# Four small tiles move ahead of the operands, a query tile gets its own place, and the first part's order gets 110 corrections

## The chip, the cores and the metric

The kernel runs on one core of a Trainium2 chip. Its time is the device time of one execution in microseconds (us), and a comparison is between medians of several executions. TensorE multiplies matrices, VectorE (DVE) and ScalarE (ACT) work on elements, GpSimd (POOL) only makes constants here, and SyncE (SP) issues every transfer between HBM and SBUF, in the order of its instruction list. An engine runs its own list in order too, and waits on semaphores for the others.

## The reference

Attention with pooled keys and values, and then a softplus feed-forward net, all in float32:

```python
k_p = k.reshape(B, H, Sp, 8, D).mean(axis=3)      # q, k, v: 8 x 8 x 576 x 64; Sp = 72
v_p = v.reshape(B, H, Sp, 8, D).mean(axis=3)
scores = 1/sqrt(D) * matmul(q, k_p.transpose(0, 1, 3, 2))
attn = exp(scores - max(scores)); attn = attn / (sum(attn) + 1e-9)
x = matmul(attn, v_p).transpose(0, 2, 1, 3).reshape(4608, 512)
h = x @ w_in                                      # 512 x 2048
g = maximum(h, 0) + log1p(exp(-abs(h)))
out = g @ w_out                                   # 2048 x 512
```

The inputs q, k, v and w_in are scaled by 8.

## The kernel before, in words

The 4608 tokens are taken in 18 chunks of 256, each of two tiles of 128 (class `Tile`). A batch has 576 tokens, so a chunk can lie in two batches. A float32 operand of the large products is split into a high part (type float32r) and a low part, and a product is three matmuls: high by high, low by high, high by low. The feed-forward net has two products for each chunk. In the first ("h" in the rows, line 494, `ffn1_products`) a 128 x 128 block of w_in is loaded as weights and x streams through, 256 columns; a pair u of two blocks of 128 hidden units takes 24 such matmuls. In the second product g is loaded and w_out streams: 512 columns in the early chunks ("acc", lines 516 and 576), and from chunk NF = 4 on ("m", line 684, `pair2_fast`) seven products of 256 columns for each pair u, with sums of quarters of g ("so") and combinations of quarters of w_out ("t"), 21 matmuls a pair.

The program has two parts, each ordered by the planner `Order`. A step is an `op`: an engine, an estimated cost, a function that emits instructions, the steps it comes after, and the `Slot`s (buffers, PSUM banks) that it needs. `run` gives each step a rank, its cost and the longest way to the end of what follows it. Then it picks step by step: of those that can start within 0.4 us of the earliest on the engine that would finish first, the one with the largest rank plus `first`. `first` is a bonus given by hand. The planner's times decide only the order; on the chip the engines wait for what they need.

The first part (`batch`, `weights`, `attend`, `feed`, `keys_values`, `combinations`) does chunks 0 to 2 and the attention of chunk 3, and meanwhile converts the 16 weight sets of w_in and w_out. `weights(f)` loads a set by SP (lines 757 and 760), and VectorE takes out its parts in six steps (`bits`, `clamp`, `shift`, `sign`, `lowest`, `rest`, lines 791 to 822) with one copy by ScalarE (`high`, line 818). `batch(b)` loads and pools keys and values for batches 0 and 1: keys in two halves (line 867, summed by TensorE on line 921), what is left over of both (lines 855 and 880), the transposes of the keys (line 219). `attend(c)` loads q of a chunk by tiles (line 308), transposes it (line 337), makes scores (line 357), their least value mn (line 364), exponentials with their sums sm (line 382), the normalized probabilities pm and pe (`norm`, lines 392 to 406), their transposes (lines 420 and 432), and x from the values (lines 461 to 478). `feed(c)` makes the two products of a chunk.

The second part does the steady chunks: in each pair u the first products of one pair, the second products of the pair before, and between them the attention of the next chunk. Weights of w_in are loaded again there from a copy in HBM (`load_wi`), and the combinations t by `load_t` through `load_sums`.

Buffers in SBUF have tags, and all tiles with one tag share its place. Places of a pool follow one another in the order in which the tags are first used, each rounded up to 32 bytes in a partition. The pools come in the order const, wpool (weights), one (nearly all else), two. In the pool `two` there are the tags mn and sm, with two places of 32 bytes each. Modulo 256, all weights begin at byte 192, and x, g, gh, gl and so at byte 0; between them lies the tile pe, whose 832 bytes are an odd multiple of 64.

Chunk 0's q lies in a tile that chunks 1 and 2 use after it; the load for chunk c comes after the transposes of the same tile of chunk c - 1 (`q_free[c - 1, t]`). There are four places "ld" of 4096 bytes (L, X4, X5, X6) for loads of keys, values and late weights.

Of the kernel before, what the change touches and what calls it, by code (L numbers as in the profile page):

```python
# [103 lines left out]
def pooled_attention_softplus_ffn(  # L104
# [19 lines left out]
    T = 2  # L124
# [14 lines left out]
    one = ctx.enter_context(tc.tile_pool(name="one", bufs=1))  # L139
    two = ctx.enter_context(tc.tile_pool(name="two", bufs=2))  # L140
    psum = ctx.enter_context(tc.tile_pool(name="psum", bufs=1, space=PSUM))
    dram = ctx.enter_context(tc.tile_pool(name="dram", bufs=1, space=bass.MemoryType.DRAM))
    BANKS = [f"b{i}" for i in range(8)]
    acc_banks, h_banks, at_banks, m_banks = [], [], [], []

    def spin(tags, shape, dtype, name):

        tags.append(tags.pop(0))
        return one.tile(shape, dtype, tag=tags[-1], name=name)

# [90 lines left out]
    def kv(b):  # L241

        engine = nc.vector
        kp, vp, st_ = [], [], {}

        def k_load(i, s):
            st = st_["k", i] = staging([SP, 2, POOL, D], "kst", s)
            nc.sync.dma_start(
                out=st, in_=k[b, 2 * i:2 * i + 2].rearrange("h (j s) d -> j h s d", s=POOL))

        def k_pool(i):
            if i == 0:
                kp.append(one.tile([SP, H, D], F32, tag="kp", name="kp"))
            tree(st_.pop(("k", i)), kp[0][:, 2 * i:2 * i + 2], engine)

        def v_load(i, s):
            st = st_["v", i] = staging([P, 2, POOL, D], "vst", s)
            for j in range(2):
                src = v[b, 4 * i + 2 * j:4 * i + 2 * j + 2].rearrange("e (y s) d -> y e s d", s=POOL)
                nc.sync.dma_start(out=st[j * KM:(j + 1) * KM], in_=src[0:KM])  # L260

        def v_pool(i):
            if i == 0:
# [25 lines left out]

# [39 lines left out]
    class Tile:  # L329
# [11 lines left out]

        def qT_out(self, ps):
            self.q = spin(Q, [P, HP, P], F32, "qT")
            nc.scalar.copy(out=self.q, in_=ps.rearrange("p (m i) -> p m i", m=HP))
# [14 lines left out]

        def least(self, j, ps):  # L360
# [15 lines left out]

        def exp_sum(self, j, ps):
# [7 lines left out]

        def sum(self):
            self.sm = two.tile([P, H], F32, tag="sm", name="sm")
            nc.vector.tensor_reduce(out=self.sm, in_=e_[self.c][:, self.t], axis=AX.X, op=ALU.add)
# [129 lines left out]

    def copy_out(c, t, tag=None):
        o = one.tile([P, DM], F32, tag=tag, name="o") if tag else spin(O, [P, DM], F32, "o")  # L520
        if t % 2 == 0:
# [185 lines left out]
    def load_wi(c, u):  # L707

        for k in range(2):
# [5 lines left out]

    kinds = {"bank": BANKS, "ld": LD, "ct": ["T0"], "kv": "a", "wg": "ab", "o": "ab", "qT": "ab", "mn": "ab",
             "sm": "ab", "E0": "a", "E1": "a", "pm": "a", "pe": "a", "kp": "a", "vp": "a", "lt_": "a",
             "pT": "a", "g": ["G0", "G1"], "gh": "ab", "gl": "ab", "h": "ab", **{x: "a" for x in late[:NS]}}
# [23 lines left out]
    def weights(f):  # L742
# [5 lines left out]
        def load(i):  # L748
            def fn():
# [8 lines left out]
                else:  # L758
                    for r in range(2):
# [22 lines left out]
        def bits(k):  # L782
# [5 lines left out]
            else:  # L788
                g = x["g", k] = spin(O, [P, 1, 4 * P], I32, "wg")
                up = x["raw", k].unsqueeze(1).rearrange("p x (n w) -> p x n w", w=2)[:, :, :, 1]  # L790
# [56 lines left out]
    def batch(b):  # L847
# [102 lines left out]
    def attend(c):  # L950
        s_lt, s_pT = Slot("lt_"), Slot("pT")
        lows, e_c = [], []
        tiles = [Tile(c, t) for t in range(T)]
        o_q, subs = [], []
        for t in range(T):
            def load(t=t):
                if 0 < c < N1:
                    qt_[c] = qt_[0]
                elif c not in qt_:
                    new_q(c)  # L960
                load_q_tile(c, t)
            o_q.append(op(SYNC, 1.4, load,
                          [] if c == 0 else [q_free[c - 1, t]] if c < N1 else
                          [q_free[c - 1, i] for i in range(T)], lag=2.4))
        norms = []
        for t, x in enumerate(tiles):
# [8 lines left out]
            o = op(ACT, act(512), lambda x=x, s=s_q: x.qT_out(s.tile), [o], [s_q, s_qT])  # L975
            ends, ss = [], [Slot("bank"), Slot("bank")]
# [3 lines left out]
            for i, s in enumerate(ss):  # L980
                d = op(DVE, 0.46, lambda x=x, i=i, s=s: x.least(i, s.tile), [p, *ends],
                       [s, s_mn])
                if c < N1:
                    def exp_sum(x=x, i=i, s=s, e=s_E[0], t=t):
# [4 lines left out]
                        x.exp_sum(i, s.tile)  # L989
                    ends.append(op(ACT, 1.2, exp_sum, [d], [s, s_mn, s_sm, *s_E], table="exp"))  # L990
# [13 lines left out]
        for x, ends, s_E, s_sm, s_pm, s_pe in norms:  # L1004
            if c == N1:
                ends = [op(DVE, 0.75, x.sum, [ex], [s_sm])]
            o = op(DVE, 1.45, x.norm, ends, [*s_E, s_sm, s_pm, s_pe])
# [21 lines left out]
    def feed(c):  # L1029
# [21 lines left out]
        if c < N1 - 1:  # L1051
            for t in range(T):
                s = Slot("o")
                h = {}

                def copy(t=t, h=h):
                    h["o"] = copy_out(c, t)
                o = op(DVE if t % 2 else ACT, 0.65, copy, [before2], [s, acc_slots[c][t]])
# [73 lines left out]
    for u in range(U1):  # L1132
        combinations(u)
    with tc.manual_schedule(engines={ACT, DVE, PE, SYNC}):
        for o in todo.run():
            o.fn()
# [6 lines left out]
    kinds = {"h": other[:2], "acc": other[2:4], "bank": other[4:], "ld": LD, "q": "a", "pT": "a", "qT": "ab", "lt_": "a",  # L1143
             "pe": "a", "mn": "ab", "sm": "ab", "E": "a", "kp": "a", "vp": "a", "S": "ab", "x": "b",
# [16 lines left out]
    def steady_attention(c):  # L1161
# [8 lines left out]
        for x in tiles:  # L1170
# [4 lines left out]
            qT_done[c].append(o)  # L1175
            o = op(ACT, act(512), lambda x=x, s=s: x.qT_out(s.tile), [o], [s, s_qT])
            last, ss = [], [Slot("bank"), Slot("bank")]
# [3 lines left out]
            for i, s in enumerate(ss):  # L1181
                last = [op(DVE, 0.46, lambda x=x, i=i, s=s: x.least(i, s.tile), [p, *last],
                           [s, s_mn])]
# [8 lines left out]
    def probabilities(c, tiles, s_E, s_lt, subs, where):  # L1192
# [4 lines left out]
        for x in tiles:  # L1197
            s_sm, s_pm, s_pe = Slot("sm"), Slot("G"), Slot("pe")
            o = op(DVE, 0.76, x.sum, [ex], [s_E, s_sm])
            o = op(DVE, 0.38, x.reciprocal, [o], [s_sm])  # L1200
# [189 lines left out]
```

## Time and profile before

| | |
|---|---|
| median of 3 runs | 917.85 us (916.7 to 921.63) |
| profiled execution | 915.2 us |
| its span, first to last instruction | 913.5 us |
| mean granted clock of TensorE | 0.994 |
| TensorE busy | 888.3 us (97%) |
| VectorE busy | 648.7 us (71%) |
| ScalarE busy | 407.3 us (45%) |
| moved by DMA | 191.12 MB, 209 GB/s |

A row of groups has line, engine, operation, out<-in, the sizes and the count, then busy us and mean ns of one, then idle time ahead of the group and what ended it. PE is TensorE's matmuls, PEld its weight loads, SPq the issuing of transfers. Because matmuls are pipelined, the mean of one is its latency; the distance between starts, or the lengths in the chain of waits, gives the rate. In that chain each row has start, length and what ran or was waited for, in order of time.

### The profile page before, as it was taken

The page shows a single profiled execution, that of the slowest core. Times are in us where ns is not written, and L with a number is a line of the kernel's source. Part 1 is how long each engine was busy: PE and PEld are TensorE (multiplying, and loading weights), DVE is VectorE, ACT ScalarE, POOL GpSimd, SP SyncE. Part 2 cuts the span into 40 slices and gives each one's busy share as a digit, 9 for nine tenths or more (in the row PEclk, how much of TensorE's full clock was granted, in tenths as well). Part 3 has the DMA queues.
Part 4 walks back from the last instruction along what each step waited for, and adds up shares of the span by engine and source line. Part 5 has one row for each costly group of instructions (what it writes and reads, how often), then busy time and mean ns, then how long its engine had stood idle before and what let it go on. Part 6 is the DMA issues. An engine that isn't in the chain of part 4 may idle for free.

```text
span 913.5 us, 20504 instructions
## 1 busy us (share of the span) xinstructions
PE 888.3 (97%) x8304; PEld 842.9 (92%) x8304; DVE 648.7 (71%) x1600; ACT 407.3 (45%) x824; POOL 2.4 (0%) x19
## 2 busy tenths in 40 slices
PE   4899999999999999999999999999999999999997
PEld 2678989888899999999999999999999999999997
DVE  4799988867877767787777755787666565747454
ACT  4765433344354544444353535453535343434332
POOL 1000000000000000000000000000000000000000
PEclk9899999999999999999999999999999999999999
DMA  8974625545789679789868866687656565746572
GB/s 234 265 255 144 211 93 187 153 158 155 261 288 270 215 208 249 222 256 238 236 208 243 245 201 198 215 252 223 222 168 222 192 208 184 230 144 233 161 238 84
DMA packets 107085, 191.12 MB, mean 209 GB/s; under 512 B 46064, under 2 KB 60400, under 8 KB 106992
## 3 DMA queue, kind: packets, MB, share of 16 engines
q1 hardware_dynamic: 106992, 189.82, 68.0%
q8 instruction: 65, 1.06, 0.5%
q14 instruction: 28, 0.23, 0.1%
HBM read 167.25 MB, written 22.54 MB: 208 GB/s over the span
## 4 chain that ended last, share of the span: by engine, by line
PE 94%; DVE 3%; DMA 1%; ACT 0%; issue 0%; SPq 0%; DVEq 0%; ACTq 0%
PE h L494 43%; PE m L684 30%; PE acc L516 7%; PE sc L357 3%; PE acc L576 3%; PE avp L461 2%; PE qTp L337 2%; PE avp L468 1%; PE ptp L420 1%; PE ltp L432 1%; DMA kvst<-in_k_dram 1%; PE kps L921 1%; DMA kvl<-in_v_dram 1%; DVE pm L397 0%; PE kvlp L880 0%
## 5 line engine op out<-in xcount | busy, mean ns | idle before, releaser
L494 PE MATMUL h<-x,w 128*128 128x256 f32 x3456 | 430.2, 279 | 0.7 <-DVE w L822 0.7
L494 PEld LDWEIGHTS h<-x,w 128*128 128x128 f32 x3456 | 414.9, 188 | 4.1 <-DVE w L822 0.9
L543 ACT ACTIVATE g<-h 128x512 f32<-128x512 f32 x120 | 71.8, 598 | 279.3 <-PE h L494 278.7
L684 PE MATMUL m<-w,so 128*128 128x256 f32 x1344 | 172.6, 278 | 0.0
L684 PEld LDWEIGHTS m<-w,so 128*128 128x128 f32 x1344 | 162.6, 188 | 0.0
L684 PE MATMUL m<-w,gh 128*128 128x256 f32 x672 | 131.9, 285 | 0.0
L594 DVE TENSOR_TENSOR sf<-g 128x128 f32<-128x128 f32 x112 | 32.8, 293 | 130.3 <-ACT g L543 129.4
L684 PEld LDWEIGHTS m<-w,gh 128*128 128x128 f32 x672 | 101.9, 188 | 1.9
L608 ACT CAST so<-sf 128x512 fp32r<-128x512 f32 x112 | 69.7, 622 | 55.4 <-DVE sf L597 54.9
L684 PE MATMUL m<-w,gl 128*128 128x256 f32 x336 | 93.7, 279 | 0.0
L613 DVE TENSOR_TENSOR so<-sf,so 128x512 fp32r<-128x512 f32 x112 | 77.4, 691 | 21.9 <-ACT so L608 21.7
L564 DVE TENSOR_TENSOR gl<-g,gh 128x384 fp32r<-128x384 f32 (+1 forms) x120 | 67.3, 561 | 0.6 <-ACT gh L557 0.5
L684 PEld LDWEIGHTS m<-w,gl 128*128 128x128 f32 x336 | 63.1, 188 | 0.0
L516 PE MATMUL acc<-w,g 128*128 128x512 f32 x192 | 60.8, 397 | 0.5 <-ACT g L499 0.5
L557 ACT ACTIVATE gh<-h 128x384 fp32r<-128x384 f32 (+1 forms) x120 | 59.2, 493 | 0.0
L499 ACT ACTIVATE g<-h 128x256 fp32r<-128x256 f32 x96 | 31.7, 382 | 59.0 <-PE h L494 52.8
L705 DVE TENSOR_TENSOR o<-o,m 128x256 f32<-128x256 f32 x98 | 39.7, 418 | 3.4 <-ACT o L697 0.6
L516 PEld LDWEIGHTS acc<-w,g 128*128 128x128 f32 x192 | 33.9, 187 | 6.9 <-ACT g L499 0.7
L364 DVE TENSOR_REDUCE mn<-sc 128x4 f32<-128x288 f32 x72 | 31.2, 452 | 10.6 <-PE sc L357 10.4
L516 PE MATMUL acc<-w,gl 128*128 128x512 f32 x96 | 38.0, 396 | 0.0
L597 DVE TENSOR_TENSOR sf<-g,sf 128x128 f32<-128x128 f32 x112 | 32.7, 292 | 3.9
L406 DVE TENSOR_TENSOR pe<-E,sm 128x96 f32<-128x96 f32 x72 | 15.2, 253 | 25.8 <-PE ltp L432 25.8
(165 smaller groups left out, 930.3 us busy)
## 6 DMA issues: line engine op xcount, KB each, us to landing
w<-wi SPq DMA_DIRECT2D x224, 512.0 KB
out_dram<-o SPq DMA_DIRECT2D x36, 256.0 KB
q<-in_q_dram SPq DMA_DIRECT2D x32, 256.0 KB
wst<-in_moe_w_in_dram SPq DMA_DIRECT2D x32, 256.0 KB
wst<-in_moe_w_out_dram SPq DMA_DIRECT2D x16, 512.0 KB
wi<-w SPq DMA_DIRECT2D x16, 512.0 KB
kst<-in_k_dram SPq DMA_DIRECT2D x24, 288.0 KB
vst<-in_v_dram SPq DMA_DIRECT2D x24, 256.0 KB
```

Source lines behind the costliest of these rows:

```text
L494: nc.tensor.matmul(out=ps[:, 0:CT], lhsT=row(w, kc), rhs=x[:, kc], start=first and kc == j == 0, stop=last and kc == KC - 1 and j == 2)
L499: nc.scalar.activation(out=g, in_=ps[:, 0:CT], func=AF.Softplus)
L516: nc.tensor.matmul(out=accs[c][t], lhsT=a[:, ts], rhs=w, start=f == 0 and j == 0, stop=f == FC - 1 and j == 2)
L543: nc.scalar.activation(out=g, in_=x.rearrange("p (b i) -> p b i", i=P), func=AF.Softplus)
L557: nc.scalar.activation(out=gh, in_=quarters(c, x.rearrange("p (b i) -> p b i", i=P)), func=AF.Softplus)
L564: nc.vector.tensor_tensor(out=gl, in0=quarters(c, g), in1=gh.bitcast(F32), op=ALU.subtract)
L594: tt(out=sf[:, 2], in0=g[:, 0], in1=g[:, 2], op=ALU.add)
L597: tt(out=sf[:, 3], in0=g[:, 3], in1=sf[:, 1], op=ALU.subtract)
L608: nc.scalar.copy(out=so[:, 0], in_=ss[c, u])
L613: nc.vector.tensor_tensor(out=so[:, 1], in0=sf, in1=so[:, 0].bitcast(F32), op=ALU.subtract)
L684: nc.tensor.matmul(out=ms[c][n], lhsT=x, rhs=y, start=u == 0 and j == 0 and n in (1, 6, 5, 4), stop=u == FP - 1 and j == 2 and n in (2, 7, ...
L705: nc.vector.tensor_tensor(out=o, in0=in0, in1=m[n], op=how)
```

## The change

Five things are changed.

- The pool `two` goes. mn and sm get tags mna, mnb, sma and smb in the pool `one`, 32 bytes each, chosen by the planner's slots. The rotating lists (`spin`) for qT, o and wg go too; the planner's slot names give the tags.
- The load of chunk 1's q takes an "ld" slot of its own and comes after nothing. Chunk 2 uses chunk 0's tile, after chunk 0's transposes (`q_free[0, t]`).
- Costs of SP steps for weights, keys and values are 1.5 in place of 1.75; SP begins at 0.8, and the table "exp" counts as loaded at the start.
- `HASTE` adds a number to `first` of 110 of the first part's steps, by index.
- In the second part `load_sums` loses `first=500`.

```diff
-    two = ctx.enter_context(tc.tile_pool(name="two", bufs=2))
-    def spin(tags, shape, dtype, name):
-        tags.append(tags.pop(0))
-        return one.tile(shape, dtype, tag=tags[-1], name=name)
...
-                self.mn = two.tile([P, 2, HP], F32, tag="mn", name="mn")
+                self.mn = one.tile([P, 2, HP], F32, tag="mn" + tag, name="mn")
...
-                self.sm = two.tile([P, H], F32, tag="sm", name="sm")
+                self.sm = one.tile([P, H], F32, tag="sm" + tag, name="sm")
...
+    todo.begin, todo.table = {SYNC: 0.8}, "exp"
...
-            return op(SYNC, 1.75, fn, slots=[stages[0 if early else i]], lag=2.2)
+            return op(SYNC, 1.5, fn, slots=[stages[0 if early else i]], lag=2.2)
...
-        o_k = [op(SYNC, 1.75, load(k, i), slots=[st[i]], lag=2.2) for i in range(2)]
-        o_v = [op(SYNC, 1.75, load(v, i), slots=[vt[i] or vt[0]], lag=2.2) for i in range(2)]
+        o_k = [op(SYNC, 1.5, load(k, i), slots=[st[i]], lag=2.2) for i in range(2)]
+        o_v = [op(SYNC, 1.5, load(v, i), slots=[vt[i] or vt[0]], lag=2.2) for i in range(2)]
...
-        o_q, subs = [], []
+        o_q, subs, s_q1 = [], [], Slot("ld")
         for t in range(T):
             def load(t=t):
-                if 0 < c < N1:
+                if c == 1 and c not in qt_:
+                    qt_[c] = one.tile([P, T, H, D], F32, tag=s_q1.name, name="q")
+                elif c == 2:
                     qt_[c] = qt_[0]
...
             o_q.append(op(SYNC, 1.4, load,
-                          [] if c == 0 else [q_free[c - 1, t]] if c < N1 else
-                          [q_free[c - 1, i] for i in range(T)], lag=2.4))
+                          [] if c < 2 else [q_free[0, t]] if c < N1 else
+                          [q_free[c - 1, i] for i in range(T)], [s_q1] if c == 1 else [], lag=2.4))
...
-                   [o_q[t], *([av[c - 1]] if c == N1 else [])], [s_q])
+                   [o_q[t], *([av[c - 1]] if c == N1 else [])], [s_q, *([s_q1] if c == 1 else [])])
...
+    HASTE = {27: -130, 29: -3, 34: -120, 36: -120, 45: 40, 46: 20, 48: -180, 55: -2, 56: -10,
+             57: -450, 58: 20, 62: -10, 64: 200, 72: -4, 73: -10, 77: -50, 82: -20, 93: 80, 94:
...
+             575: -140, 583: 30, 610: -20, 620: 4, 635: -80, 638: -310, 641: 40}
+    for i, x in HASTE.items():
+        todo.ops[i].first += x
...
-               lag=2.4, first=500))
+               lag=2.4))
```

More of the change, by code (lines that the diff above doesn't have):

```diff
@@ L251, in k_pool @@
         def k_pool(i):
-            if i == 0:
+            if not kp:
                 kp.append(one.tile([SP, H, D], F32, tag="kp", name="kp"))
@@ L262, in v_pool @@
         def v_pool(i):
-            if i == 0:
+            if not vp:
                 vp.append(one.tile([P, HP, D], F32, tag="vp", name="vp"))
@@ L340, in qT, with qT_out @@
                     identity=ident)
-        def qT_out(self, ps):
-            self.q = spin(Q, [P, HP, P], F32, "qT")
+        def qT_out(self, ps, tag):
+            self.q = one.tile([P, HP, P], F32, tag=tag, name="qT")
             nc.scalar.copy(out=self.q, in_=ps.rearrange("p (m i) -> p m i", m=HP))
@@ L358, in scores, with least @@
                                          rhs=kT[b % 2][js, m], start=True, stop=True)
-        def least(self, j, ps):
+        def least(self, j, ps, tag):
             if j == 0:
-                self.mn = two.tile([P, 2, HP], F32, tag="mn", name="mn")
+                self.mn = one.tile([P, 2, HP], F32, tag="mn" + tag, name="mn")
             nc.vector.tensor_reduce(out=self.mn[:, j], in_=self.view(ps), axis=AX.X, op=ALU.min)
@@ L375, in less, with exp_sum @@
                     [P, 2, 2, SP]), op=ALU.subtract)
-        def exp_sum(self, j, ps):
+        def exp_sum(self, j, ps, tag):
             if j == 0:
-                self.sm = two.tile([P, H], F32, tag="sm", name="sm")
+                self.sm = one.tile([P, H], F32, tag="sm" + tag, name="sm")
             for m in range(HP):
@@ L384, in exp_sum, with sum @@
                                      accum_out=self.sm[:, h:h + 1])
-        def sum(self):
-            self.sm = two.tile([P, H], F32, tag="sm", name="sm")
+        def sum(self, tag):
+            self.sm = one.tile([P, H], F32, tag="sm" + tag, name="sm")
             nc.vector.tensor_reduce(out=self.sm, in_=e_[self.c][:, self.t], axis=AX.X, op=ALU.add)
@@ L517, in ffn2, with copy_out @@
                                  start=f == 0 and j == 0, stop=f == FC - 1 and j == 2)
-    def copy_out(c, t, tag=None):
-        o = one.tile([P, DM], F32, tag=tag, name="o") if tag else spin(O, [P, DM], F32, "o")
+    def copy_out(c, t, tag):
+        o = one.tile([P, DM], F32, tag=tag, name="o")
         if t % 2 == 0:
@@ L713, in load_wi @@
             wi[f] = w[:, 0], w[:, 1]
-    kinds = {"bank": BANKS, "ld": LD, "ct": ["T0"], "kv": "a", "wg": "ab", "o": "ab", "qT": "ab", "mn": "ab",
+    kinds = {"bank": BANKS, "ld": LD, "ct": ["T0"], "kv": "a", "wg": "ab", "o": O, "qT": Q, "mn": "ab",
              "sm": "ab", "E0": "a", "E1": "a", "pm": "a", "pe": "a", "kp": "a", "vp": "a", "lt_": "a",
@@ L788, in bits @@
             else:
-                g = x["g", k] = spin(O, [P, 1, 4 * P], I32, "wg")
+                g = x["g", k] = one.tile([P, 1, 4 * P], I32, tag=gslot[k].name, name="wg")
                 up = x["raw", k].unsqueeze(1).rearrange("p x (n w) -> p x n w", w=2)[:, :, :, 1]
@@ L972, in attend @@
             o = op(PE, 0.5, lambda x=x, s=s_q: x.qT(bank(s, "qTp")),
-                   [o_q[t], *([av[c - 1]] if c == N1 else [])], [s_q])
+                   [o_q[t], *([av[c - 1]] if c == N1 else [])], [s_q, *([s_q1] if c == 1 else [])])
             q_free[c, t] = o
-            o = op(ACT, act(512), lambda x=x, s=s_q: x.qT_out(s.tile), [o], [s_q, s_qT])
+            o = op(ACT, act(512), lambda x=x, s=s_q, n=s_qT: x.qT_out(s.tile, n.name), [o], [s_q, s_qT])
             ends, ss = [], [Slot("bank"), Slot("bank")]
@@ L980, in attend, with exp_sum @@
             for i, s in enumerate(ss):
-                d = op(DVE, 0.46, lambda x=x, i=i, s=s: x.least(i, s.tile), [p, *ends],
+                d = op(DVE, 0.46, lambda x=x, i=i, s=s, n=s_mn: x.least(i, s.tile, n.name), [p, *ends],
                        [s, s_mn])
                 if c < N1:
-                    def exp_sum(x=x, i=i, s=s, e=s_E[0], t=t):
+                    def exp_sum(x=x, i=i, s=s, e=s_E[0], t=t, n=s_sm):
                         if c == 0 and 0 not in e_:
@@ L988, in exp_sum @@
                         x.slot = e.name
-                        x.exp_sum(i, s.tile)
+                        x.exp_sum(i, s.tile, n.name)
                     ends.append(op(ACT, 1.2, exp_sum, [d], [s, s_mn, s_sm, *s_E], table="exp"))
@@ L1005, in attend @@
             if c == N1:
-                ends = [op(DVE, 0.75, x.sum, [ex], [s_sm])]
+                ends = [op(DVE, 0.75, lambda x=x, n=s_sm: x.sum(n.name), [ex], [s_sm])]
             o = op(DVE, 1.45, x.norm, ends, [*s_E, s_sm, s_pm, s_pe])
@@ L1054, in feed, with copy @@
                 h = {}
-                def copy(t=t, h=h):
-                    h["o"] = copy_out(c, t)
+                def copy(t=t, h=h, s=s):
+                    h["o"] = copy_out(c, t, s.name)
                 o = op(DVE if t % 2 else ACT, 0.65, copy, [before2], [s, acc_slots[c][t]])
@@ L1142, in pooled_attention_softplus_ffn @@
     other = [b for b in BANKS if b not in acc_banks]
-    kinds = {"h": other[:2], "acc": other[2:4], "bank": other[4:], "ld": LD, "q": "a", "pT": "a", "qT": "ab", "lt_": "a",
+    kinds = {"h": other[:2], "acc": other[2:4], "bank": other[4:], "ld": LD, "q": "a", "pT": "a", "qT": Q, "lt_": "a",
              "pe": "a", "mn": "ab", "sm": "ab", "E": "a", "kp": "a", "vp": "a", "S": "ab", "x": "b",
@@ L1175, in steady_attention @@
             qT_done[c].append(o)
-            o = op(ACT, act(512), lambda x=x, s=s: x.qT_out(s.tile), [o], [s, s_qT])
+            o = op(ACT, act(512), lambda x=x, s=s, n=s_qT: x.qT_out(s.tile, n.name),
+                   [o], [s, s_qT])
             last, ss = [], [Slot("bank"), Slot("bank")]
@@ L1181, in steady_attention @@
             for i, s in enumerate(ss):
-                last = [op(DVE, 0.46, lambda x=x, i=i, s=s: x.least(i, s.tile), [p, *last],
+                last = [op(DVE, 0.46, lambda x=x, i=i, s=s, n=s_mn: x.least(i, s.tile, n.name), [p, *last],
                            [s, s_mn])]
@@ L1198, in probabilities @@
             s_sm, s_pm, s_pe = Slot("sm"), Slot("G"), Slot("pe")
-            o = op(DVE, 0.76, x.sum, [ex], [s_E, s_sm])
+            o = op(DVE, 0.76, lambda x=x, n=s_sm: x.sum(n.name), [ex], [s_E, s_sm])
             o = op(DVE, 0.38, x.reciprocal, [o], [s_sm])
```

10 rows, old and new, of the table HASTE are left out of this document.

## The prediction

> **What bounds the kernel now.** The page of the profile comes first: the busy row of the engines and the chain that ended last, in a span of 913.5 us.
>
> ```profile
> PE 888.3 (97%) x8304; PEld 842.9 (92%) x8304; DVE 648.7 (71%) x1600; ACT 407.3 (45%) x824; POOL 2.4 (0%) x19
> ...
> PE 94%; DVE 3%; DMA 1%; ACT 0%; issue 0%; SPq 0%; DVEq 0%; ACTq 0%
> ```
>
> TensorE is the bound: 94% of the chain is its own work. Time can come only from its idle 25.2 us (913.5 - 888.3) or from the rate of its matmuls. A table of stages shows where the idle part is (columns: busy us of each engine with instruction counts, granted clock, DMA share, GB/s).
>
> ```profile
> 0.00:55.00 55.00, 37.49 (x419) 26.70 (x419) 35.22 (x75) 34.78 (x135) 2.37 (x19) 0.91 0.88 240
> 55.00:82.00 27.00, 24.87 (x239) 21.24 (x239) 25.00 (x47) 14.18 (x27) 0.00 (x0) 1.00 0.60 195
> 82.00:905.00 823.00, 822.22 (x7620) 791.50 (x7618) 584.16 (x1470) 357.39 (x661) 0.00 (x0) 1.00 0.68 209
> 905.00:913.50 8.50, 3.69 (x32) 3.49 (x30) 4.33 (x11) 0.99 (x2) 0.00 (x0) 0.96 0.16 62
> ```
>
> Idle is 17.5 us before 55 and 2.1 us from 55 to 82, then 0.8 us up to 905; the last 4.8 us are the output's tail, which the change leaves alone. So the first part's list works on at most 19.6 us, and the 823 us from 82 to 905 answer only to the matmul rate. What the first 82 us wait for, by groups (the last column is idle time before the group and its releaser):
>
> ```profile
> L921 PE MATMUL kps<-kvst,zm 128*64 128x256 f32 x20 | 7.8, 540 | 9.6 <-DVE kvst L914 6.0 <-DMA kvst<-in_k_dram 3.7
> L357 PE MATMUL sc<-kT,qT 64*64 64x72 f32 x256 | 6.7, 252 | 1.6 <-ACT kT L225 1.6
> ...
> L337 PE MATMUL qTp<-ident,q 128*128 128x128 f32 x32 | 4.8, 286 | 1.5 <-DMA q<-in_q_dram 1.5
> ...
> L432 PE MATMUL ltp<-ident,pe 128*96 128x128 f32 x16 | 3.2, 281 | 4.9 <-DVE pe L406 4.9
> ```
>
> The 6.0 is the start (first data, then VectorE's sums) and stays. The 3.7, 1.5 and 1.6 us hang on transfers and keys, the 4.9 us on VectorE. The chain over this stretch says why the 3.7 us wait ends so late:
>
> ```profile
> 12.82 0.37 SPq L308
> 13.19 0.05 issue
> 13.24 0.88 SPq L757
> 14.11 0.05 issue
> 14.16 6.41 DMA kvst<-in_k_dram
> 20.57 0.14 issue
> 20.70 3.65 PE kps L921 x8
> ```
>
> It runs through the DMA queue's load of chunk 1's q (L308) to the key load of batch 1, for which TensorE waits until 20.70.
>
> **Part 1: chunk 1's q gets a place of its own.** Before, it reuses chunk 0's tile, so its load waits for q_free[0, t], the transposes. SP issues in order:
>
> ```profile
> 6.15 1.75 SPq L760 DMA_DIRECT2D wst<-in_moe_w_in_dram  x2
> 12.07 1.11 SPq L308 DMA_DIRECT2D q<-in_q_dram  x2
> ```
>
> SP stands still from 7.90 (6.15 + 1.75) to 12.07, 4.2 us, and behind it wait the w_out half of weight set 0, both key halves of batch 1, batch 0's values and batch 1's leftovers. The transfers themselves ran dry meanwhile (last but one column):
>
> ```profile
> 8.00:10.00 2.00, 1.79 (x2) 0.32 (x2) 0.00 (x0) 0.00 (x0) 0.00 (x0) 1.00 1.26 243
> 10.00:12.00 2.00, 2.00 (x9) 1.07 (x9) 1.37 (x2) 0.58 (x1) 0.00 (x0) 1.00 0.45 142
> 12.00:14.00 2.00, 1.76 (x69) 1.52 (x72) 0.20 (x1) 1.90 (x5) 0.00 (x0) 1.00 0.35 80
> ```
>
> Against 1.26 the two middle stretches left (0.81 + 0.91) x 2 / 1.26 = 2.7 us of transfer time unused. So everything behind that load lands 2.7 to 4.2 us earlier: 2.7 if the engines are the limit, 4.2 if the queue is. The new place is one of the four "ld" slots. Three hold batch 0's key halves and leftovers, and q of chunk 1 is the fourth, so batch 1's loads now wait for the products that read batch 0's halves out of theirs; that is why I take 3.0 us, near the lower end. It counts in full as far as the path through 20.70 goes on to the first weights: VectorE too waits on this queue, 2.81 us for the w_out of set 0:
>
> ```profile
> 19.12 0.69 DVE L791 TENSOR_SCALAR wg<-wst 128x1024 int32<-128x1024 int32 x1 [2.81 <-DMA wst<-in_moe_w_out_dram]
> ...
> 20.89 0.69 DVE L397 TENSOR_TENSOR pm<-E,sm 128x512 f32<-128x512 f32 x1
> ...
> 28.18 1.23 DVE L813 SCALAR_TENSOR_TENSOR wg<-wst,wg 128x1024 int32<-128x1024 int32 x1
> ```
>
> If that cover is gone, because another transfer takes the freed time, the part is worth 0.
>
> **Part 2: corrections to the ranks (HASTE), with the load costs 1.75 to 1.5, the queue's start at 0.8 and the "exp" table taken as loaded.** No instruction is added or removed; only the order of the first part's steps changes. By index, 27, 34 and 36 are batch 1's leftover products, first key products and key transposes on TensorE (-130, -120, -120), so chunk 0's attention goes ahead of them. Now it goes behind: its first probabilities are written at 20.89 (above), and TensorE transposes them here, ten microseconds later:
>
> ```profile
> 31.04 0.60 PE L420 MATMUL ptp<-ident,pm 128*128 128x128 f32 x4
> ```
>
> Most other entries reorder VectorE's six conversion steps of a weight set against the attention and the split of g. What they can win is the idle time left once part 1 is in: 4.9 + 1.6 = 6.5 us. Not all of it: VectorE is busy 25.00 of 27 us from 55 to 82, so there only its order can change, not its amount. I take 3.0 us, somewhat under half. The bounds are 6.5 us gained, and 2.5 us lost, if two of VectorE's long steps (1.23 us each, L813 above) get in front of a normalization that TensorE waits for.
>
> **Part 3: addresses.** The two mn and two sm tiles, 32 bytes each, leave the last pool and get their place at their first use, in chunk 0's attention: ahead of lt_, pT, x, g, gh, gl and so. These move up by 4 x 32 = 128 bytes; the weights, in an earlier pool, stay. Modulo 256 the weights begin at 192 and x, g and the sums at 0, so 64 above; after, at 128, 64 below. In the first products the weights are loaded and x streams, in the second ones g or so is loaded and weights stream: the two kinds have opposite signs already. A steady chunk in the chain (start, length):
>
> ```profile
> 497.21 2.83 PE h L494 x24
> 500.04 2.39 PE m L684 x21
> 502.43 2.72 PE h L494 x24
> 505.16 2.48 PE m L684 x21
> ...
> 541.97 2.48 PE m L684 x21
> 544.45 0.59 PE h L494 x5
> ```
>
> Identical runs have two lengths: 2.83 or 2.72 us for 24 (118 or 113 ns each), 2.48 or 2.39 for 21. Both signs show the same pair of rates, so exchanging the signs should change neither, and I take 0. The bounds come from these lengths. From 497.21 to 544.45 the 8 h runs are 5 slow and 3 fast, the 8 m runs 2 slow and 6 fast. All fast: 5 x 0.11 + 2 x 0.09 = 0.73 us a chunk, 10.2 us over 14 chunks, and up to 3.5 us more for the four chunks before those, whose 768 h matmuls (32 times 24, by 0.11) show the slow form, as in this row of the whole chain:
>
> ```profile
> 214.19 2.83 PE h L494 x24
> ```
>
> That makes 13.7 us gained. All slow: 3 x 0.11 + 6 x 0.09 = 0.87 us, 12.2 us lost.
>
> The Trainium skill, "SBUF — State Buffer", "Who interferes with whom", gives TensorE two independent read ports, one for the streamed operand and one for weight loads, and has it wait for nobody. By that rule an address can't matter and this part is exactly 0. The rows neither need nor confirm it: two lengths for the same run show a state that the rule doesn't have.
>
> **Part 4: the rest.** Named slots in place of the spin lists, named mn and sm: the same copies on the same engines, 0. load_t loses its lead of 500 on SP. They are covered: TensorE idles 0.8 us in the 823 us from 82; if the t loads came late the wait would show where chunk 4's second products begin. Bounds 0 to 3.2 us lost (one 256 KB load late by half the 6.41 us in which the 512 KB key load above landed), taken as 0.
>
> **Sum.** -3.0 - 3.0 + 0 + 0 = -6.0 us. The profiled execution took 915.2 us, 1.7 around its span of 913.5; 909.2 follows. The median of the runs, 917.85, lies 2.65 above that execution, so 911.9 for the median (-0.65%).
>
> **Rivals.** *Addresses make runs fast* (for: the two lengths exist, and fast costs nothing else; against: both signs show both). All fast gives 911.9 - 13.7 = 898.2, half of it 905. *The early gain is swallowed* (for: VectorE at 25.00 of 27 us from 55 to 82 makes the weights, and transfers at 0.88 share before 55 deliver them; TensorE starts earlier and then waits for set 2 or 3; against: VectorE had 20 us free before 55): at most 1 us stays, 917. *Addresses make runs slow* (the other side): every h and m run of the 14 steady chunks takes the long form, +12.2 on the -6.0 of the list: 924. It outweighs the list once over half of the fast runs (6.0 of 12.2) turn. For it: slow is what the first four chunks take; against: as above. *The stall is not removed*, because q of chunk 1 now waits for its slot: parts 2 and 3 alone, 915; it belongs with the swallowed case.
>
> **Chances.** Forecast 0.56, own range 908 to 915.5 (part 1 from 4.2 to 1.5, part 2 from 5.7 to 1); addresses fast 0.13; swallowed or not removed 0.22; addresses slow 0.09. A measurement of this kernel tells about 0.5%, 4.6 us, from no change: faster means under 913.3. Of the forecast 0.43 of its 0.56 lies there, with 0.13 of the fast case: 0.56. Within: 0.13 + 0.20 = 0.33. Slower: 0.09 + 0.02 = 0.11. The range reaches to half of the fast case and past the swallowed one: 903 to 920.
>
> **What would show it.** Part 1: SP's gap of 4.2 us ahead of the second q load is gone, DMA share over 1 from 8 to 14, batch 1's key products before 18. Part 2: TensorE's idle before 82 is 12 to 14 us in place of 19.6, and the steady chunks begin some 6 us earlier. Part 3: lengths of 2.83/2.72 and 2.48/2.39 in the old proportion, and 8 pairs in 47.2 us; any other proportion makes it wrong. The forecast falls if a steady chunk changes by more than 0.2 us (2.8 us over 14), or if idle turns up after 82.

## The result and the profile after

The changed kernel takes 904.41 us (median of 4 runs, 903.13 to 905.2), the kernel before, run beside it, 919.74 (916.7 to 923.04). The ratio is 0.9838, with a 95% interval of 0.9809 to 0.9867: faster by 1.3 to 1.9%. Beside the other runs below, the kernel before had medians of 917.06 to 917.61 (13 to 29 runs each). The forecast was 911.9, with 908 to 915.5 as its own range and 903 to 920 with the rivals: 904.41 lies in the second and not in the first. Two medians below are of nine runs in place of ten, because one run in each of these two sets took far longer (1,769 us with only the place of chunk 1's q, whose median with it is 912.7, and 1,102 us with one correction left out). The profiled execution took 903.13 us around a span of 901.4, so the span is 12.1 us shorter; 6.0 were forecast.

First the page's busy row and chain, then the table by stages (columns as before; its third row ends 12 us earlier, since the span does):

```profile
PE 883.9 (98%) x8304; PEld 840.9 (93%) x8304; DVE 648.7 (72%) x1600; ACT 407.5 (45%) x824; POOL 2.4 (0%) x19
...
PE 95%; DVE 2%; DMA 1%; SPq 1%; ACT 1%; issue 0%; DVEq 0%; ACTq 0%
```

```profile
0.00:55.00 55.00, 42.51 (x513) 30.53 (x514) 40.41 (x84) 37.70 (x140) 2.37 (x19) 1.00 0.98 278
55.00:82.00 27.00, 26.81 (x208) 23.93 (x207) 26.29 (x48) 14.70 (x30) 0.00 (x0) 1.00 0.48 147
82.00:893.00 811.00, 811.00 (x7560) 783.02 (x7559) 577.74 (x1460) 354.08 (x654) 0.00 (x0) 1.00 0.68 211
893.00:901.40 8.40, 3.61 (x31) 3.40 (x29) 4.22 (x10) 0.99 (x2) 0.00 (x0) 0.94 0.17 62
```

TensorE's idle before 82 is 12.5 + 0.2 = 12.7 us, where it was 19.6. That is 6.9 of the 12.1. From 82 on there is no idle, and the tail is as before. The granted clock up to 55 went from 0.91 to 1.00.

Where the rest lies is seen from the steady chunks' second products. Their rows by operation give the first and the last start, before and now:

```profile
L684 PE MATMUL m<-w,gh x672: 276/280/386, 256.6 to 908.3; 128*128 128x256 f32 x168
L684 PE MATMUL m<-w,gl x336: 276/278/286, 256.8 to 908.4; 128*128 128x256 f32 x168
...
L678 PE MATMUL m<-w,gh x672: 276/279/388, 243.9 to 896.2; 128*128 128x256 f32 x168
L678 PE MATMUL m<-w,gl x336: 276/279/285, 244.1 to 896.3; 128*128 128x256 f32 x168
```

They begin 12.7 us earlier and take as long as before: 652.4 us from the first start to the last, against 651.8 (256.6 to 908.4). So the whole gain is made before 244 us. Of the 12.7 us, 6.9 are idle time before 82, and 0.5 are idle time between 82 and 240, of which the changed kernel has none:

```profile
82.00:240.00 158.00, 157.46 (x1142) 140.92 (x1141) 134.66 (x255) 66.30 (x146) 0.00 (x0) 1.00 0.52 168
```

The other 5.3 us are faster matmuls. The groups before 82 say which waits went:

```profile
L351 PE MATMUL sc<-kT,qT 64*64 64x72 f32 x256 | 6.5, 230 | 0.7 <-ACT qT L338 0.3 <-ACT kT L219 0.2
L916 PE MATMUL kps<-kvst,zm 128*64 128x256 f32 x20 | 6.1, 438 | 6.8 <-DVE kvst L909 6.0 <-DMA kvst<-in_k_dram 0.8
L331 PE MATMUL qTp<-ident,q 128*128 128x128 f32 x32 | 5.3, 303 | 2.5 <-DMA q<-in_q_dram 2.5
...
L426 PE MATMUL ltp<-ident,pe 128*96 128x128 f32 x16 | 3.4, 289 | 0.3 <-DVE pe L400 0.3
```

The wait for keys fell from 3.7 to 0.8 us, that for `pe` from 4.9 to 0.3, that for `qT` and `kT` from 1.6 to 0.7; the wait for q rose from 1.5 to 2.5. But SyncE's gap is still there. Its list (start, length, line), which before stood still from 7.90 to 12.07:

```profile
6.19 1.74 SPq L755 DMA_DIRECT2D wst<-in_moe_w_in_dram  x2
7.97 0.47 SPq L752 DMA_DIRECT2D wst<-in_moe_w_out_dram  x1
13.40 0.37 SPq L302 DMA_DIRECT2D q<-in_q_dram  x1
13.81 0.58 SPq L862 DMA_DIRECT2D kvst<-in_k_dram  x1
```

It stands from 8.44 to 13.40, 5.0 us. By the program's order the load at 13.40 isn't chunk 1's: it is the second tile of chunk 2, which reuses chunk 0's tile and waits for chunk 0's transposes. The transfers run dry as before, now in one stretch (their share from 10 to 12 is 1.05), and batch 1's key products come at 18.01 in place of 20.70:

```profile
12.00:14.00 2.00, 2.00 (x42) 1.71 (x40) 0.00 (x0) 1.49 (x4) 0.00 (x0) 1.00 0.07 27
```

```profile
18.01 1.91 PE L916 MATMUL kps<-kvst,zm 128*64 128x256 f32 x8 [0.75 <-DMA kvst<-in_k_dram]
```

What moved ahead of the gap is one transfer, the w_out half of weight set 0, issued at 7.97 in place of 13.24; VectorE starts on it at 15.19 in place of 19.12.

The corrections, for their part, put chunk 0's attention ahead of batch 1's leftover products. TensorE transposes its first probabilities at 22.27, where before it did so at 31.04 (and at 26.96 in the changed kernel without the corrections):

```profile
22.27 0.60 PE L414 MATMUL ptp<-ident,pm 128*128 128x128 f32 x4
```

The clock is the first part of the 5.3 us. Before, three stretches had a low granted clock (the last column but two); after, none has:

```profile
18.00:21.00 3.00, 0.29 (x1) 0.29 (x2) 1.78 (x5) 2.52 (x13) 0.00 (x0) 0.59 1.06 366
21.00:25.00 4.00, 4.00 (x32) 2.10 (x34) 1.53 (x4) 0.00 (x0) 0.00 (x0) 0.50 1.20 270
...
36.00:40.00 4.00, 4.00 (x77) 3.11 (x81) 3.36 (x6) 3.81 (x19) 0.00 (x0) 0.63 1.06 331
```

Behind the wait of 3.7 us that ended at 20.70, TensorE worked 4 us at half its clock; the eight key products took 3.65 us there and 1.91 us after. The Trainium skill, "TensorE: Matmul & The Clock Gate", "What's actually happening", has the clock halve after an idle window of about 3.4 us and come back after as much work; the 3.7 us wait and the 0.50 agree. The low clock from 36 to 40 stands behind two shorter waits, of 0.7 and 1.4 us. As an estimate from these clocks, if every matmul there lost by the clock, the busy time of the two longer stretches holds 4.0 x 0.50 + 4.0 x 0.37 = 3.5 us of loss, which the sum didn't have; the runs leave about 2 us for it (below).

The other part is the rate of the first products. One run of 24 of them, from the chain of waits of the changed kernel at about the time of the row shown of before (2.83), with the steady chunk beside it:

```profile
214.52 2.74 PE h L488 x24
...
489.69 2.73 PE h L488 x24
492.42 2.38 PE m L678 x21
494.80 2.83 PE h L488 x24
497.63 2.48 PE m L678 x21
```

Before the steady chunks the mean distance between starts of these matmuls went from 117.7 to 114.8 ns: 29 of 800 had the short distance (around 113) before, 568 after. In the steady chunks the two lengths are still there, in another proportion (2,405 of 4,868 distances were over 115.5 ns before, 2,685 of 4,869 now) and with other neighbours: before, a long h run was followed by a short m run and a short h by a long m; now short goes with short and long with long.

### The profile page after: what moved, and what is told of

It reads as the page before. It is cut to its first block, busy times and chain, and to the rows that moved or that the text cites. A ratio compares the mean times of both kernels' runs of the same rounds, so it can differ in the third digit from the quotient of the medians.

```text
span 901.4 us, 20496 instructions
## 1 busy us (share of the span) xinstructions
PE 883.9 (98%) x8304; PEld 840.9 (93%) x8304; DVE 648.7 (72%) x1600; ACT 407.5 (45%) x824; POOL 2.4 (0%) x19
## 4 chain that ended last, share of the span: by engine, by line
PE 95%; DVE 2%; DMA 1%; SPq 1%; ACT 1%; issue 0%; DVEq 0%; ACTq 0%
PE h L488 44%; PE m L678 31%; PE acc L510 7%; PE acc L570 3%; PE sc L351 2%; PE avp L455 2%; PE qTp L331 2%; PE ptp L414 2%; PE avp L462 1%; DMA wst<-in_moe_w_out_dram 1%; PE ltp L426 1%; DMA kvl<-in_v_dram 1%; ACT E L376 0%; SPq L302 0%; DVE o L699 0%
```

## Experiments on the parts of the change

**Old addresses in the new order.** The order of the program is the changed kernel's; mn and sm go to a last pool again, so x, g and the sums begin at 0 modulo 256.

```diff
+    two = ctx.enter_context(tc.tile_pool(name="two", bufs=1))
-                self.mn = one.tile([P, 2, HP], F32, tag="mn" + tag, name="mn")
+                self.mn = two.tile([P, 2, HP], F32, tag="mn" + tag, name="mn")
...
```

> The changed kernel with its whole order, but the mn and sm tiles back in a pool behind everything, so that x, g and the sums begin at 0 modulo 256 as before (weights at 192). Theory S (the sign of the address distance sets which runs are fast): all h runs of the first part go back to 118 ns a matmul and the 512-column ones to 233, the first part gets 3.6 us longer (539 h matmuls by 4.4 ns and 185 of 512 columns by 6.7), the steady part 0.6 to 1.2 us shorter: 2.4 to 3 us above the changed kernel, near 907. Rival O (the order alone made the runs fast): 904.4, and the first part's h runs stay at 113. The recorded prediction (addresses are worth 0) expects 904.4 as well.

Measured: 907.63 us, ratio to before 0.9902 (0.9868 to 0.9937), span 904.8. Idle before 82 is 12.9 us, as with the new addresses, and the clock is 1.00; the second products begin at 247.3 in place of 243.9. The first products are long again:

```profile
0.00:55.00 55.00, 42.18 (x513) 30.33 (x514) 40.45 (x84) 37.61 (x140) 2.36 (x19) 1.00 0.99 278
55.00:82.00 27.00, 26.91 (x206) 23.94 (x206) 26.29 (x48) 14.43 (x29) 0.00 (x0) 1.00 0.47 150
```

```profile
204.76 2.83 PE h L489 x24
...
210.39 2.83 PE h L489 x24
```

The rows agree with Theory S, and rival O falls. So the addresses are worth 3.4 us of span, 3.2 by the medians, all before the steady chunks: 800 first products by 2.8 ns are 2.3 us, and 384 second products of 512 columns by 3.5 ns (233.3 to 229.8) are 1.3. It also splits the 12.7 us: order and q's place give 256.6 - 247.3 = 9.3, of which 19.6 - 12.9 = 6.7 are idle time before 82, 0.5 idle time after it, and 2.1 are left for the clock.

**New addresses in the old order.** The kernel before, with mn and sm in the pool `one` by slot names, and no other part.

```diff
-    two = ctx.enter_context(tc.tile_pool(name="two", bufs=2))
-                self.mn = two.tile([P, 2, HP], F32, tag="mn", name="mn")
+                self.mn = one.tile([P, 2, HP], F32, tag="mn" + tag, name="mn")
...
```

> The kernel before with its order, only the mn and sm tiles moved ahead of pT, lt_, x, g and the sums, which so begin at 128 modulo 256 as in the changed kernel. Theory S: h runs of the first part near 113 ns, 512-column ones near 227, 3 us less in the first part, 0.6 to 1.2 us more in the steady part: 2 to 3 us below the kernel before, 915 to 916, and in the steady part the order of long and short runs of the changed kernel. Rival O and the recorded prediction: no change, 917.9.

Measured: 916.6 us, ratio 0.9996 (0.997 to 1.0021): no change that the runs can tell, as the prediction had it, but not for its reason. The first products went to 114.6 ns and the second products begin at 253.7 in place of 256.6, 2.9 us earlier. The steady part took it back: it is 2.6 us longer, of which 0.7 is a wait of the scores for VectorE; the second products' mean distance went from 115.3 to 116.0 ns, which over 2,352 of them is 1.6. So the gain in the first chunks belongs to the addresses in both orders; what the steady chunks make of it depends on the order.

**Only the place of chunk 1's q.** The kernel before, with the "ld" slot and chunk 2 after chunk 0.

```diff
+                if c == 1 and c not in qt_:
+                    qt_[c] = one.tile([P, T, H, D], F32, tag=s_q1.name, name="q")
+                elif c == 2:
...
```

> The kernel before with chunk 1's q in an ld place of its own, nothing else. The recorded prediction's part 1: SP's 4.2 us gap ahead of that load goes, -3.0 us, 915. Rival: the new place is itself still being read when the load is due, SP stands as long as before (in the changed kernel it stands 5.0 us there), so 0, 917.9, or up to 2 us more if other loads lose their place.

Measured: 912.33 us, ratio 0.9958 (0.9932 to 0.9984), 5.1 us under before by the medians; the ratio makes it 3.9, and its interval 1.5 to 6.2. The profiled span is 3.2 us shorter. Here SyncE's gap is gone, as the prediction said, and two waits on TensorE came up in its stead:

```profile
7.90 0.47 SPq L757 DMA_DIRECT2D wst<-in_moe_w_out_dram  x1
8.41 0.43 SPq L867 DMA_DIRECT2D kvst<-in_k_dram  x1
8.97 1.81 SPq L308 DMA_DIRECT2D q<-in_q_dram  x2
```

```profile
L357 PE MATMUL sc<-kT,qT 64*64 64x72 f32 x256 | 6.9, 254 | 4.6 <-ACT qT L344 3.2 <-ACT kT L225 1.4
...
L432 PE MATMUL ltp<-ident,pe 128*96 128x128 f32 x16 | 3.4, 299 | 3.6 <-DVE pe L406 2.4 <-ACT pT L427 1.2
```

The transfers run on without a break, and batch 1's key products start at 14.75:

```profile
12.00:14.00 2.00, 2.00 (x41) 1.68 (x39) 0.00 (x0) 1.45 (x4) 0.00 (x0) 1.00 1.11 337
```

```profile
14.75 1.94 PE L921 MATMUL kps<-kvst,zm 128*64 128x256 f32 x8
```

The DMA waits for keys and q, 3.7 + 1.5 us, are gone; ScalarE's `qT` and `kT` took 3.0 of it (1.6 to 4.6). The longest of the new waits, 3.23 us for `qT` up to 20.94, comes with a granted clock of 0.50 from 20.0 to 26.9. Idle before 82 is 16.4 us, 3.2 less.

**The place taken back out of the changed kernel.** Corrections and addresses stay.

```diff
-                          [] if c < 2 else [q_free[0, t]] if c < N1 else
-                          [q_free[c - 1, i] for i in range(T)], [s_q1] if c == 1 else [], lag=2.4))
+                          [] if c == 0 else [q_free[c - 1, t]] if c < N1 else
+                          [q_free[c - 1, i] for i in range(T)], lag=2.4))
...
```

> The changed kernel with the load of chunk 1's q put back: it goes into chunk 0's tile after chunk 0's transposes; the corrections and the addresses stay. If the place is worth in the corrected list what it gave alone (917.4 to 912.7), the time is about 909 and TensorE's idle before 82 some 4 us more than 12.7. Rival: in the corrected list SyncE stands 5.0 us ahead of this load anyway, so the place gives nothing and the time stays within 1 us of 904.4.

Measured: 908.83 us, ratio 0.9898 (0.9856 to 0.994), span 906.8, 5.4 over the changed kernel's. The place is worth in the corrected list about what it is worth alone, though SyncE stands still in both. Idle before 82 is 15.5 + 0.2 = 15.7 us, 3.0 more, and the clock up to 55 falls to 0.94. SyncE's list shows the difference:

```profile
11.78 1.29 SPq L302 DMA_DIRECT2D q<-in_q_dram  x2
13.12 0.58 SPq L752 DMA_DIRECT2D wst<-in_moe_w_out_dram  x1
13.75 0.48 SPq L862 DMA_DIRECT2D kvst<-in_k_dram  x1
```

The key load goes out when it does in the changed kernel (13.75 against 13.81), but with 512 KB of w_out 0.6 us ahead of it; TensorE then waits 2.2 us for it in place of 0.8. So in the corrected list the place works through what is sent into the gap, not by closing it. That is a reading of the two lists up to 20 us; behind that the planner orders other steps differently too.

**No corrections.** The changed kernel without the loop that applies `HASTE`.

```diff
-    for i, x in HASTE.items():
-        todo.ops[i].first += x
```

> The changed kernel without the 110 corrections to the ranks. Addresses, q's place, costs and begin stay. The recorded prediction put the corrections at 3.0 us: 907.4. Theory L (the corrections carry nearly all that the order is worth, some 9 us): 912 to 914, with TensorE idle 18 us or more before 82 and granted clock below 0.95 before 55.

Measured: 914.94 us, ratio 0.9974 (0.9945 to 1.0003), span 910.1: the corrections are worth 10.5 us by the medians, 8.7 by the spans. Idle before 82 is 14.4 + 1.7 = 16.1 us, 3.4 more than with them, and the second products begin 3.4 us later. The other 5.3 us are lost behind that, in the steady part, which takes 658.0 us in place of 652.7. Most of them are in a stretch with 3.0 us idle and a lower clock: the chain runs through a load of values that took 10.99 us, the scores wait 2.7 us for VectorE up to 292.4, and the clock is 0.50 for the next 3.4 us.

```profile
245.00:300.00 55.00, 52.05 (x491) 50.37 (x490) 36.94 (x96) 21.25 (x39) 0.00 (x0) 0.97 0.88 237
```

```profile
276.27 10.99 DMA vst<-in_v_dram
```

Theory L had nearly the time, but not the place: idle before 82 stays under its 18 us, and the clock before 55 is 1.00. Neither the kernel before (652.1 us in the steady part) nor the one with the place alone (652.2) has this loss, and the one with the new addresses alone has half of it (654.7). So a part of what the corrections are worth here undoes a loss that the other parts of the change make together; the load costs, SyncE's begin, the table and `load_sums` without its lead were not run by themselves.

**One correction left out.** Of the 110 entries, number 302 (+50) is the one on chunk 2's second q load, for which SyncE stands still in the changed kernel.

```diff
-             1090, 285: -50, 286: 230, 289: -10, 295: -10, 297: 670, 302: 50, 308: -4, 316: -10,
+             1090, 285: -50, 286: 230, 289: -10, 295: -10, 297: 670, 308: -4, 316: -10,
```

> The changed kernel with one of the 110 corrections left out, entry 302 (+50): it lifts chunk 2's load of its second q tile, which needs chunk 0's transposes, ahead of batch 1's first key load. Without it SyncE does not stand from 8.44 to 13.40. If that gap is on the path, as the prediction has it for part 1, the key load goes out at 8.4 in place of 13.8, batch 1's first key products run some 5 us earlier, and the time is 900 to 902. Rival: TensorE has other work meanwhile (it waits only 0.8 us for these keys in the changed kernel) and the rest of the list is fitted to this order, so the gap costs nothing and its removal brings new waits, as in the kernel without any correction, where sc waits 4.3 and ltp 3.5 us: 905 to 912, idle before 82 above 14 us.

Measured: 919.12 us, ratio to before 1.002 (0.9987 to 1.0053). The whole gain of the change is gone with one number. The gap did close (the key load goes out at 8.36), and TensorE waits for no transfer of keys or q any more. But the other 109 entries now meet another order. Idle before 82 is 15.7 us, and further on TensorE waits up to 90.7 for VectorE, which took conversion steps ahead of the low part of g; a half clock comes with it, from 89.7 to 96.6:

```profile
PE acc L510 <- DVE gl L499: 3.5, 1, 3.5
```

```profile
82.00:90.00 8.00, 5.18 (x31) 4.24 (x30) 7.77 (x10) 2.37 (x5) 0.00 (x0) 0.98 0.92 279
90.00:96.00 6.00, 5.30 (x19) 4.51 (x20) 5.51 (x8) 1.05 (x1) 0.00 (x0) 0.50 0.87 307
```

My theory, that the gap costs up to 5 us here, fell; the rival has the direction right and its size (905 to 912) too small.

## Experiments on the addresses

In these the address of the streamed operand less that of the loaded one, modulo 256, is varied: x less w_in in the first products (h), w_out less g in the second (m). The changed kernel has -64 for h and +64 for m. The first four fix the order of the places in the pool `one` by tiles that nothing uses, which moves other tiles too (pT, lt_, the loads); their second products begin at 246.2 to 248.2, so 2 to 4 us of each belong to the first part. The last two put 32 or 96 bytes ahead of the pool; theirs begin at 248.8, 4.9 us later than the changed kernel's.

```diff
+    for tag, n in (("X01", 2048), ("X23", 2048), ("gha", 384), ...):   # the order differs by run
+        one.tile([P, n], F32, tag=tag, name="place")
```

```diff
+    one.tile([P, 8], F32, tag="pad", name="pad")        # 24 in the other run
```

> The same with x, g and the sums at 192 as the weights, distance 0. Theory S has no row for it. If the two forms come from the streamed reads and the weight loads meeting in one place, distance 0 is the worst: a third, longer form over 118 ns for 256 columns, 5000 steady matmuls by 4 ns or more: over 924. If only the sign of a distance matters, near 904.

> The same with x, g and the sums at 64, 128 from the weights modulo 256. If the pattern repeats every 128 bytes, the same as distance 0; if every 256, it is a third case of its own: all short (about 890) if the greatest distance is best, else between 904 and 917.

> The changed kernel, instructions and order untouched; only places move. For both kinds of product the streamed operand lies 64 below the loaded one modulo 256: x at 128 with the weights at 192 (h), weights at 192 with g and the sums at 0 (m). Theory S, read from the four traces so far: a run that starts after other work takes the short form when the streamed operand is 64 below and the long one when it is 64 above; a passage from below to above keeps the form, from above to below switches it. With both below, runs start short, and if a passage between equal signs keeps the form, nearly all 2685 long steady matmuls get shorter by 4.4 ns: 11.8 us below the changed kernel, 892 to 893. If such a passage switches it: near 904. Rival N (the form alternates with the count of passages, the signs only set its start): 904, with about half of the runs long.

> The same with both streamed operands 64 above the loaded ones: x at 0, g and the sums at 128, weights at 192. Theory S: runs start long after other work; if equal signs keep the form, all are long: 2184 short steady matmuls by 4.4 ns are 9.6 us more, and 3.6 us in the first part: near 917. Rival N: 904 to 908.

> The changed kernel with 32 bytes of padding ahead of everything in the pool `one`, so x, g and the sums begin at 160 modulo 256 and the weights at 192: 32 apart in place of 64. Theory that only the side counts: as the changed kernel, about 904.5, the first products before the steady chunks at 114.8 ns, the two lengths 113.3 and 117.8 ns a matmul. Rival, that the two lengths belong to a distance of 64 bytes: 32 is between 0 (120.0 ns everywhere, 926 in the run with distance 0) and 64, and the time lies above 912.

> The same with 96 bytes of padding: x, g and the sums at 224 modulo 256, 32 above the weights. If only the side counts: as the changed kernel with the old addresses, about 907.6, 3.2 slower than 32 below, the first products at 117.6 ns. If 64 bytes matter: above 912 and near the run with 32 below.

Measured; the third column is the mean distance between starts of h matmuls before the steady chunks, the fourth the time from the start of the first m run to the end of the last, both from the starts in the trace. In the steady part of all these runs TensorE is idle for at most 0.3 us and its clock is 1.00, so the fourth column is the rate of the matmuls and not the order:

| run | h / m, bytes | h before, ns | steady part, us | median, us | ratio to before |
|---|---|---|---|---|---|
| changed kernel | -64 / +64 | 114.8 | 652.7 | 904.41 | 0.9838 |
| old addresses | +64 / -64 | 117.6 | 652.7 | 907.63 | 0.9902 |
| both below | -64 / -64 | 116.1 | 654.0 | 907.68 | 0.9886 (0.9834 to 0.9937) |
| both above | +64 / +64 | 117.1 | 660.2 | 913.35 | 0.9942 (0.9918 to 0.9966) |
| 32 above | +32 / -32 | 116.8 | 661.2 | 916.37 | 0.9992 (0.997 to 1.0015) |
| 32 below | -32 / +32 | 118.3 | 660.9 | 916.99 | 0.9988 (0.9966 to 1.0011) |
| 128 | 128 / 128 | 119.3 | 665.1 | 920.23 | 1.0019 (0.9994 to 1.0045) |
| 0 | 0 / 0 | 119.5 | 671.5 | 926.06 | 1.0102 (1.0072 to 1.0131) |

Single runs of 24 and 21 in the chain show it for distance 0 and, below it, for both above:

```profile
494.37 2.88 PE h L491 x24
497.25 2.52 PE m L681 x21
```

```profile
500.33 2.83 PE h L491 x24
503.16 2.48 PE m L681 x21
```

A distance of 64 bytes with opposite sides is worth 18.8 us of the steady part against 0 and about 8.4 against 32. At 128 neither expectation held: the time is between that of 0 and that of 64. With 32 the side made no difference (0.6 us between the medians) and short runs were rare: the rival of that experiment was right, the theory that only the side counts wrong. With 64 the short length needs streamed operands that lie below in at least one of the products: with both above, 4,526 of 4,869 steady distances were long (over 115.5 ns). With both below the time didn't fall to the 892 of an all-short steady part; 907.68 is nearer the 904 written for the case that the form changes from run to run. One half of Theory S fits the sequences at 64 with opposite sides without exception, counted over the runs of five and more matmuls in the changed kernel: passing from a run with the streamed operand below straight to one above keeps the length (56 of 56), from above to below changes it (71 of 71). The other half holds only in the main: after other work, 27 of 39 first-product runs (operand below) started short and 36 of 55 second-product runs (above) long; with both below, 15 of 39 first-product runs started short. It is read off the traces, and why TensorE would do so isn't shown.

## Why the prediction was right and where it was wrong

**The range held partly by luck.** The mechanism that was forecast, less idle time before 82, came true at about its size: 6.9 us for 6.0. The span fell by twice the forecast, because of two terms that the sum had at nothing: the addresses (3.4 us) and the clock (about 2). 904.41 is outside the forecast's own range, and inside the whole one only because that reached to half of a rival, fast addresses. The addresses gave a quarter of that rival's 13.7 us, and none of it in the steady chunks, where most of the 13.7 was to come from.

**The sign, the place and the idle time were right.** 12 to 14 us of idle before 82 were named as the sign of parts 1 and 2, and it is 12.7. The steady chunks begin 12.7 us earlier, though, where some 6 were named. "If idle turns up after 82": none did. A steady chunk changed by 0.6 / 14 = 0.04 us, under the 0.2 that was the limit.

**Part 1: the size held, the mechanism only in part.** The working was that SyncE's 4.2 us gap goes and that all behind it lands earlier, 3.0 us. Alone the place gave 5.1 by the medians, 3.9 by the ratio and 3.2 by the spans; taken out of the corrected list it gave 4.4 by the medians and 5.4 by the spans. That is about the bounds of 2.7 to 4.2, and the runs don't tell more exactly. Alone the gap does go, and about 3 us come back as waits on ScalarE. Its three signs all hold for the place alone: no gap, a DMA share of 1.24, 1.07 and 1.11 from 8 to 14, and the key products at 14.75 in place of 20.70. In the changed kernel none of the three holds: the gap stays, the share from 12 to 14 is 0.07, and the key products start at 18.01, not before 18, though 2.7 us earlier than in the kernel before. The rival "the stall is not removed" had the fact right, for another reason (chunk 2's q waits there, not chunk 1's), but its 915 assumed that an open gap means no gain, and the run without the place says otherwise. The step that failed is the reading of one wait as the path: what counted in the changed kernel was that w_out of set 0 went ahead of the gap and out of the key load's way.

**Part 2 was right as idle time and too small as time.** In its own terms, the order once part 1 is in, it is the step from the run with the place alone to the run with the old addresses: 910.3 to 904.8, 5.5 us of span (4.7 by the medians), where 3.0 stood with a bound of 6.5. Idle time before 82 falls by 3.5 of that (16.4 to 12.9) and by 0.5 behind it. The term that was left out is the slow clock, 0.50 from 20.0 to 26.9 with the place alone and 1.00 up to the tail with the old addresses. The reading of the entries was right in the main: chunk 0's attention went ahead (22.27 in place of 31.04); entry 34 is on the second half of batch 1's key products, not the first. Taken out last, the corrections are worth more, 10.5 by the medians and 8.7 by the spans, because a worse list makes waits further on (3.0 us between 245 and 300 without any correction, 3.5 us near 87 without one of them), which a bound from the first 82 us can't hold. By the spans, the place is worth 3.2 put in first and 5.4 taken out last; the order is worth 5.5 put in after the place, and the corrections 8.7 taken out last.

**Part 3 was wrong in its reason.** "Both signs show the same pair of rates, so exchanging the signs should change neither" holds for the sum of the steady chunks, 652.7 us with either sign, because there the two kinds trade: with the old signs in the same order 992 first-product distances are short, not 1,157, and 1,202 second-product ones, not 945. The old proportion, which was named as the sign, did not stay. It fails for the chunks before, where the signs gave 117.6 and 114.8 ns: -3.4 us. The prediction's own bound, 3.5 us for the first four chunks, had the right place, and its size by luck: it counted 768 first products, all turning short, where 568 of 800 did (2.3 us), and not the second products of 512 columns (1.3). It was listed as part of a rival. That half of that rival's effect gives 905, near the 904.41, is a coincidence too. The rule of the Trainium skill, "SBUF — State Buffer", "Who interferes with whom", that TensorE waits for nobody, read as the prediction read it, would make all the address runs equal. They differ by 18.8 us of steady time with the same instructions, so here the measurement decides against that reading. Where the two reads meet, if they do, no run here shows.

**Part 4** shows nothing in the changed kernel: no idle at the start of chunk 4. `load_t` without its lead was not tried by itself.

**The sum** of the span: 6.9 us less idle before 82, 0.5 less between 82 and 240, 3.4 by the addresses and 1.9 that is left for the clock, less the 0.6 by which the steady chunks got longer: 12.1. The forecast had the first of these, at 6.0.

## What to carry to other kernels

A wait on TensorE can cost more than itself. Waits of 3.7, 3.2 and 2.7 us each came with a granted clock of 0.50 for 3.4 to 6.8 us, so price that as well. The length alone doesn't decide it: waits of 0.7 and 1.4 us close together came with 0.50 in the kernel before (36 to 40), and waits of 2.4 and 0.5 us left the clock at 1.00 in the run without corrections (17.6 to 21.2). An order worked out with many corrections is worth something only as a whole: find out what a stall covers before it is removed, since one entry here decided over 13.3 us of the span. When runs of identical matmuls show two lengths, look at the places of both operands modulo 256 before calling it noise.

## What the runs showed that I had not expected

Matmuls of 256 columns with the same instructions have spacings that depend on how far the streamed operand lies from the loaded one modulo 256 bytes: 119.9 ns on average at 0, about 118.5 at 128, some 117 to 118 at 32, and 113.3 or 117.8 at 64, where which of the two comes depends on the side and on the run before. In the steady part that is 671.5, 665.1, 661 and, at 64, 652.7 to 660.2 us. Other distances were not tried. That the pattern repeats after 256 bytes is not shown either, only that it doesn't after 128, since 0 and 128 differ.

A single correction to the planner's ranks moved the time by 14.7 us (904.41 to 919.12), more than the whole change had been forecast to give.
